# Scaling the attention weights by 1/sum on ScalarE, two units at a time, in place of a product on TensorE behind the values

## The chip, the cores and the metric

The kernel runs on one core of a Trainium2 chip. The core has five engines with queues of their own: TensorE (PE in the profile; PEld is its weight load), VectorE (DVE), ScalarE (ACT), GpSimd (POOL) and SyncE (SP, which issues the DMAs). The metric is the device time of one execution in microseconds (us). The kernel before took 731.99 us, the median of three runs from 730.23 to 732.29. One profiled execution of it took 733.05 us, and its profiled span is 731.3 us.

## The reference

Attention with four sink tokens and a window of 128, followed by a feed forward with a squared ReLU. The attention's output, its 8 heads side by side, is the feed forward's input.

```python
scores = scale * np.matmul(q, k.transpose(0, 1, 3, 2))   # q, k, v: (4, 8, 768, 64)
keep = is_sink | in_window          # pos < 4, or 0 <= row - pos < 128
scores = np.where(keep, scores, -1000000000.0)
scores = scores - np.max(scores, axis=-1, keepdims=True)
a = np.exp(scores)
a = a / (np.sum(a, axis=-1, keepdims=True) + 1e-09)
attn = np.matmul(a, v)              # then heads side by side: x is (3072, 512)
h = x @ w_in                        # w_in: (512, 2048), w_out: (2048, 512)
r = np.maximum(h, 0.0)
g = s * (r * r) + b
return g @ w_out
```

## The kernel before

**Chunks.** The 3072 tokens are worked in 8 chunks of 384 tokens, half a sequence each, in the order `ORDER`. For each chunk the attention is computed and then the feed forward. While the feed forward of chunk c runs, the attention of chunk c+1 is issued between its steps. Chunks 0 and 1 take their attention from a class of its own (`Plain`), which has its own normalisation; chunks 2 to 7 are built by `attn_slots`, and it is those that are meant by "from the third chunk on".

**Exactness by splits.** Products that must be exact to more bits than one pass of TensorE keeps are made of several: a value is cast to a rounded part and a rest (`kh` and `kl`, the two parts of `hl`, `x[0]` and `x[1]`, the two parts of `g`), and the products of the parts are added up in PSUM. So one feed-forward step is either 12 products `h<-x,w` of 128x384 (l1, line 608) or 9 products `po<-w,g` of 128x512 (l2, line 628), 16 steps of each kind per chunk, in turn.

**Units.** `attn_slots` cuts a chunk's attention into 24 units, one per head and block of 128 queries. A slot t issues the pieces of several units at different stages: the scores of unit t (`unit_a`: two products at lines 309 and 310, the mask, scale and negative maximum on DVE at 314, the exponential with its sum on ACT at 320, on POOL the addition at 323 of two 128x128 squares of the tile `sm` into one, and at 324 a copy of the sinks' exponentials into the tile `psk`); the transpose of unit t+1-LB into the spare columns of a PSUM bank (`turn`, line 330); the split of unit t-LB (`unit_b`: 343 on DVE, 345 on ACT, 346 on POOL); and the values' products of unit t-LC (`unit_c`: lines 375 and 383, and per head 390 and 391). LB is 4 and LC is 7, so a unit's transpose comes three slots behind its scores.

**Where 1/sum comes in.** The transposes and values' products work on exponentials that are not yet divided. Per pair of heads, behind the pair's last `unit_b`, 1/sum is computed on DVE for six columns (355 to 359) and written into spare columns of `psk`. `psk` of four heads is transposed (`ts`, 398) and copied to `xsk` (400, 401). From it `sinks` computes the sinks' part of the output (product `os`, 407; addition 408), and `scaled` spreads 1/sum over the rows with a constant selector (product `zb` with `sel`, 414) and multiplies the output with it on DVE (415), after which 416 and 417 split it for the feed forward.

**The order.** The slots of a chunk are spread over the feed forward's 32 steps: a step is issued, then slots as long as `i * (len(steps) - 2) < (j + 1) * len(slots)`. There are 33 slots for 30 places, so three steps take two slots each. The tile framework then sets each engine's queue from this text and its own estimates; an instruction that is wrapped in `tc.keep_in_program_order` keeps its place relative to the others so wrapped. Each engine works its queue in order. PSUM has five banks in the pool `psA` (scores with transposes, `h`, `o`, `ts`, `os`, `zb`) and three for `po`.

Of the kernel before, what the change touches and what calls it, by code (L numbers as in the profile page):

```python
# [15 lines left out]
P = 128  # L16
B, H, S, D = 4, 8, 768, 64
ORDER = ((0, 0), (1, 0), (0, 1), (1, 1), (2, 0), (2, 1), (3, 0), (3, 1))
NS = 8
# [18 lines left out]
LB, LC, LD, LDL, L2 = 4, 7, ((3, 4), (6, 7)), ((2, 2), (3, 3)), 2  # L38
# [3 lines left out]
def tile_kernel(ctx, tc, qT, kT, k0, v, vsk, n_sink, window, w, s, b, out):  # L42
# [46 lines left out]
    sel = const.tile([P, 2, P], F32R, tag="sel", name="sel")  # L89

# [43 lines left out]
    def constants2():  # L134

        spread = wk.tile([P, 2, P], F32, tag="y", name="spread", bufs=3)
        nc.gpsimd.memset(spread, 0.0)
        for j in range(4):
            row = spread[96:P, j // 2].rearrange("p (a d) -> p a d", a=2)
            nc.gpsimd.affine_select(out=row, in_=row, pattern=[[1, 2], [0, D]], compare_op=ALU.not_equal, fill=1.0,  # L140
                                    base=2 * j, channel_multiplier=-1)
        nc.scalar.copy(sel, spread)
# [102 lines left out]
    def load_pair(k, pr):  # L245
# [15 lines left out]
        pp.zz = wk.tile([P, BLK, 2], F32, tag="zz", name="zz", bufs=2)  # L261
# [36 lines left out]
    def unit_a(k, h, i, sc):  # L298
# [10 lines left out]
        nc.tensor.matmul(sc[:, :n], hd.qs[:, qs], hd.kh[:, c0:c0 + n], start=True, stop=False)  # L309
        nc.tensor.matmul(sc[:, :n], hd.qs[:, qs], hd.kl[:, c0:c0 + n], start=False, stop=True)  # L310
# [7 lines left out]
        s0 = k.cc[(h, i)][3]  # L318
        hh = h % 2
        nc.scalar.activation(sm[:, :n], sm[:, :n], AF.Exp, bias=negm[:, uu], scale=-1.0, accum_out=pp.zz[:, i, hh:hh + 1])  # L320
        if g > 0:
            c1, p1 = k.cc[(h, i)][1:3]
            nc.gpsimd.tensor_tensor(out=sm[:, c1:c1 + P], in0=sm[:, p1:p1 + P], in1=sm[:, c1:c1 + P], op=ALU.add)  # L323
        nc.gpsimd.tensor_copy(out=pp.psk[:, i, :12 * NS].rearrange("p (t x) -> p t x", t=3)[:, :, h % 4 * NS:(h % 4 + 1) * NS],  # L324
                              in_=sm[:, s0:s0 + NS].unsqueeze(1).to_broadcast([P, 3, NS]))

    def turn(k, h, i, tp):

        sm, c0 = k.cc[(h, i)][:2]
        nc.tensor.transpose(tp, sm[:, c0:c0 + P], ident)  # L330

    def unit_b(k, h, i, tp):
# [17 lines left out]
        pp = k.pairs[h // 2]  # L350
        if h % 2 == 1 and i == BLK - 1:
            z0 = 12 * NS + h // 2 % 2 * 4
            zr = wk.tile([P, 2, BLK, 2], F32, tag="zr", name="zr")
            zh = wk.tile([P, BLK, 2], F32R, tag="zh", name="zh")
            nc.vector.tensor_scalar(out=zr[:, 0], in0=pp.zz, scalar1=1e-9, scalar2=None, op0=ALU.add)
# [63 lines left out]
    def attn_slots(c):  # L419
# [16 lines left out]
        def slot(t):  # L436
            def f():
# [9 lines left out]
                if 0 <= t - LB < n:  # L447
                    unit_b(k, *units[t - LB], k.bank[:, 3 * P:])
# [399 lines left out]
```

## Time and profile before

| | |
|---|---|
| three runs, us | 732.29, 730.23, 731.99 |
| profiled execution, us | 733.05 |
| its span, us | 731.3 |
| matmuls on PE | 3812, 96% busy |
| DVE, ACT, POOL busy | 69%, 65%, 56% |
| products of the feed forward (608 and 628) | 297.7 and 299.1 us busy |
| DMA | 52.62 MB, mean 72 GB/s |

A row of instructions names the line, the engine, the operation and out<-in by the program's names. Matmuls are pipelined: one that is listed with 343 ns starts well before the one ahead of it has its end listed, so what a product costs PE is read from the distance between starts, and not from its duration. The feed forward of chunk 0 starts at about 44.5 us; the weights are still being prepared until about 123 us, and from 150.8 us on the stages repeat: one feed forward of some 82 to 86 us each (starts at 150.8, 237.0, 322.3, 404.7, 490.0, 572.3 and 657.0), the last of them without attention beside it.

### The profile page before, as it was taken

The numbers are of one execution on the slowest core, as the hardware profiler recorded it, in microseconds if no ns is written. First come the engines' busy times: TensorE is split into PE (matmuls) and PEld (weight loads), VectorE is DVE, ScalarE is ACT, GpSimd is POOL, SyncE is SP. The second block draws the span as 40 slices with busy tenths as digits, with TensorE's granted clock in tenths as the row PEclk, the third lists the DMA queues.
The fourth block names the chain that finished last, engine by engine and source line by source line (L and its number), as shares of the span: only waits on it lengthen the run. The fifth ranks groups of instructions, "written<-read, shape, count | busy, mean of one in ns | idle before, by whom it ended". The sixth has DMA issues, their size and how long they took to land.

```text
span 731.3 us, 11917 instructions
## 1 busy us (share of the span) xinstructions
PE 700.8 (96%) x3812; PEld 617.5 (84%) x3812; DVE 508.2 (69%) x1202; ACT 473.5 (65%) x1157; POOL 410.8 (56%) x703
## 2 busy tenths in 40 slices
PE   7599898999999999999999999999999999999996
PEld 4267666889988999899998999899999999989895
DVE  6969988548985788657786588847787589743331
ACT  6978877467774687656784677747775577633222
POOL 2556886348892588716674488915765389810000
PEclk8889988999999999999999999999999999999999
DMA  7845031131210212111111222111111212000001
GB/s 289 333 173 216 12 137 37 52 103 48 89 56 24 90 56 63 34 62 54 45 58 49 75 70 63 45 51 51 57 52 56 72 42 69 3 19 26 0 1 48
DMA packets 27381, 52.62 MB, mean 72 GB/s; under 512 B 3504, under 2 KB 15536, under 8 KB 25392
## 3 DMA queue, kind: packets, MB, share of 16 engines
q1 hardware_dynamic: 27312, 51.79, 21.3%
q8 instruction: 32, 0.52, 0.3%
q14 instruction: 37, 0.30, 0.1%
HBM read 45.49 MB, written 6.29 MB: 71 GB/s over the span
## 4 chain that ended last, share of the span: by engine, by line
PE 78%; DVE 9%; POOL 7%; ACT 3%; issue 2%; DMA 0%; SPq 0%; POOLq 0%; ACTq 0%; DVEq 0%
PE h L608 32%; PE po L628 32%; POOL w L206 4%; PE o L383 3%; PE sc L309 2%; PE sc L310 2%; PE sc L330 2%; DVE w L220 1%; PE tp L550 1%; PE o L561 1%; DVE smf L538 1%; DVE wt L219 1%; PE o L375 1%; POOL hl L346 1%; POOL kl L290 1%
## 5 line engine op out<-in xcount | busy, mean ns | idle before, releaser
L608 PE MATMUL h<-x,w 128*128 128x384 f32 x1536 | 297.7, 343 | 6.7 <-ACT tf L552 3.4
L628 PE MATMUL po<-w,g 128*128 128x512 f32 x1152 | 299.1, 405 | 0.0
L608 PEld LDWEIGHTS h<-x,w 128*128 128x128 f32 x1536 | 266.4, 189 | 13.1 <-ACT tf L552 3.8
L628 PEld LDWEIGHTS po<-w,g 128*128 128x128 f32 x1152 | 211.9, 191 | 45.6 <-issue 2.1
L614 DVE SCALAR_TENSOR_TENSOR r<-h,sb,r 128x384 f32<-128x384 f32 x112 | 68.9, 615 | 78.8 <-ACT r L611 77.7
L611 ACT ACTIVATE r<-h 128x384 f32<-128x384 f32 x128 | 62.6, 489 | 91.8 <-PE h L608 82.6
L617 DVE SCALAR_TENSOR_TENSOR g<-r,sb,g 128x384 fp32r<-128x384 f32 x112 | 91.1, 814 | 31.1 <-ACT g L616 29.6
L346 POOL TENSOR_TENSOR hl<-two,hl 128x256 fp32r<-128x256 f32 x128 | 102.3, 800 | 15.5 <-ACT hl L345 12.9
L323 POOL TENSOR_TENSOR sm<-sm 128x128 f32<-128x128 f32 x128 | 67.3, 526 | 60.9 <-ACT sm L320 59.1
L320 ACT ACTIVATE sm<-sm,negm 128x264 f32<-128x264 f32 (+1 forms) x144 | 72.1, 501 | 28.6 <-DVE negm L314 27.3
L616 ACT ACTIVATE g<-r,sb 128x384 fp32r<-128x384 f32 x112 | 69.1, 617 | 22.7 <-DVE r L614 22.0
L290 POOL TENSOR_TENSOR kl<-kraw,kh 128x528 fp32r<-128x528 f32 (+1 forms) x48 | 60.3, 1257 | 19.1 <-ACT kh L288 18.8
L206 POOL TENSOR_TENSOR w<-w 128x256 int32<-128x256 int32 x60 | 45.0, 780 | 40.3 <-DVE w L220 32.0
L345 ACT CAST hl<-two 128x256 fp32r<-128x256 f32 x128 | 50.5, 395 | 25.8 <-DVE two L343 25.5
L343 DVE TENSOR_TENSOR two<-sc,split 128x256 f32<-128x256 f32 x128 | 53.1, 417 | 5.8 <-POOL hl L346 5.5
L324 POOL COPY psk<-sm 128x24 f32<-128x24 f32 x144 | 35.5, 246 | 17.1 <-ACT sm L320 17.0
L383 PE MATMUL o<-hl,vv 128*128 128x256 f32 (+1 forms) x256 | 44.3, 275 | 0.0
L383 PEld LDWEIGHTS o<-hl,vv 128*128 128x128 f32 x256 | 39.6, 188 | 3.2
L289 DVE TENSOR_TENSOR qs<-qraw,qs 64x384 fp32r<-64x384 f32 x48 | 39.6, 825 | 3.7 <-ACT qs L285 1.9
L314 DVE CUSTOM_DVE_ANT_0 sm<-sc,m_all 128x264 f32<-128x264 f32 x64 | 27.3, 426 | 21.2 <-PE sc L310 19.2
L314 DVE CUSTOM_DVE_ANT_0 sm<-sc,msk 128x264 f32<-128x264 f32 (+1 forms) x80 | 32.0, 400 | 14.1 <-PE sc L310 13.4
L309 PE MATMUL sc<-kh,qs 128*128 128x264 f32 (+1 forms) x144 | 41.6, 291 | 0.0
(138 smaller groups left out, 960.4 us busy)
## 6 DMA issues: line engine op xcount, KB each, us to landing
w<-in_w SPq DMA_DIRECT2D x15, 1024.0 KB, 8.8
kraw<-in_kT SPq DMA_DIRECT2D x32, 264.0 KB, 2.6
out<-ot SPq DMA_DIRECT2D x24, 256.0 KB, 2.0
qraw<-in_qT SPq DMA_DIRECT2D x24, 192.0 KB, 2.4
vraw<-in_v SPq DMA_DIRECT2D x16, 256.0 KB, 2.8
kraw<-in_kT SPq DMA_DIRECT2D x16, 200.0 KB, 2.5
vsraw<-in_vsk SPq DMA_DIRECT2D x24, 64.0 KB, 2.1
vraw<-in_v SPq DMA_DIRECT2D x8, 192.0 KB, 2.4
```

What stands on the lines that cost most here:

```text
L206: nc.gpsimd.tensor_tensor(out=out[q], in0=in0[q], in1=in1[q], op=op)
L290: nc.gpsimd.tensor_tensor(out=hd.kl[:, :kw], in0=hd.k[:, :kw], in1=hd.kh[:, :kw].bitcast(F32), op=ALU.subtract)
L320: nc.scalar.activation(sm[:, :n], sm[:, :n], AF.Exp, bias=negm[:, uu], scale=-1.0, accum_out=pp.zz[:, i, hh:hh + 1])
L323: nc.gpsimd.tensor_tensor(out=sm[:, c1:c1 + P], in0=sm[:, p1:p1 + P], in1=sm[:, c1:c1 + P], op=ALU.add)
L346: nc.gpsimd.tensor_tensor(out=lo, in0=both, in1=hi.bitcast(F32), op=ALU.subtract)
L383: nc.tensor.matmul(hd.o[:, q0:q0 + n * P], hd.vv[:, kb, :], hd.hl[:, t, c0 * P:(c0 + n) * P], start=(hd.n == 0), stop=(i == BLK - 1 and kb ...
L608: nc.tensor.matmul(h[:, :CH], weight[f][:, 0, wi, cc * P:(cc + 1) * P], x[xi][:, cc, :], start=(i == 0), stop=(i == 11))
L611: nc.scalar.activation(r, h[:, :CH], AF.Relu, scale=1.0 / WUP)
L614: nc.vector.scalar_tensor_tensor(out=hr, in0=h[:, :CH], scalar=sw_ap, in1=r, op0=ALU.mult, op1=ALU.mult)
L616: nc.scalar.activation(gg[:, 0, :], hr, AF.Identity, bias=b_ap, scale=1.0)
L617: nc.vector.scalar_tensor_tensor(out=gg[:, 1, :], in0=hr, scalar=b_ap, in1=gg[:, 0, :].bitcast(F32), op0=ALU.add, op1=ALU.subtract)
L628: nc.tensor.matmul(po[tb], gg[:, gi, tsl], weight[f][:, 1, wi, :], start=(f == 0 and i == 0), stop=(f == NF - 1 and i == 2))
```

## The change

1/sum no longer goes through TensorE. A new function `norm` is called in every even slot for the two units whose scores were issued in the two slots before. It computes 1/sum of those two units on DVE (an addition and a reciprocal over two columns), multiplies each unit's added 128x128 square by it in place on ScalarE, and on POOL the former copy of the sinks' exponentials into `psk` becomes a multiplication by the same factor. The transposes, the values' products and the sinks' product then work on divided weights. `scaled`, its 24 products and multiplications, the constant `sel`, and the six-column computation per pair are gone; the two lines that split the output move to the end of `sinks`. One slot per chunk is gone, so there are 32 slots for 30 places and two steps take two slots. All products of `attn_slots` and of the feed forward are wrapped in `tc.keep_in_program_order`: besides those shown, the values' products, the transposes of `psk` and the product `os`.

```diff
-LB, LC, LD, LDL, L2 = 4, 7, ((3, 4), (6, 7)), ((2, 2), (3, 3)), 2
+LB, LC, LD, LDL, L2 = 4, 7, (3, 5), (2, 2), 2
...
-    sel = const.tile([P, 2, P], F32R, tag="sel", name="sel")
...
-        spread = wk.tile([P, 2, P], F32, tag="y", name="spread", bufs=3)
-        nc.gpsimd.memset(spread, 0.0)
-        for j in range(4):
-            row = spread[96:P, j // 2].rearrange("p (a d) -> p a d", a=2)
-            nc.gpsimd.affine_select(out=row, in_=row, pattern=[[1, 2], [0, D]], compare_op=ALU.not_equal, fill=1.0,
-                                    base=2 * j, channel_multiplier=-1)
-        nc.scalar.copy(sel, spread)
...
-        pp.zz = wk.tile([P, BLK, 2], F32, tag="zz", name="zz", bufs=2)
+        pp.z = wk.tile([P, 3, 2 * BLK], F32, tag="zz", name="zz", bufs=2)
...
-        nc.tensor.matmul(sc[:, :n], hd.qs[:, qs], hd.kh[:, c0:c0 + n], start=True, stop=False)
-        nc.tensor.matmul(sc[:, :n], hd.qs[:, qs], hd.kl[:, c0:c0 + n], start=False, stop=True)
+        tc.keep_in_program_order(nc.tensor.matmul(sc[:, :n], hd.qs[:, qs], hd.kh[:, c0:c0 + n], start=True, stop=False))
+        tc.keep_in_program_order(nc.tensor.matmul(sc[:, :n], hd.qs[:, qs], hd.kl[:, c0:c0 + n], start=False, stop=True))
...
-        s0 = k.cc[(h, i)][3]
-        hh = h % 2
-        nc.scalar.activation(sm[:, :n], sm[:, :n], AF.Exp, bias=negm[:, uu], scale=-1.0, accum_out=pp.zz[:, i, hh:hh + 1])
+        nc.scalar.activation(sm[:, :n], sm[:, :n], AF.Exp, bias=negm[:, uu], scale=-1.0,
+                             accum_out=pp.z[:, 0, h % 2 * BLK + i:h % 2 * BLK + i + 1])
         if g > 0:
             c1, p1 = k.cc[(h, i)][1:3]
             nc.gpsimd.tensor_tensor(out=sm[:, c1:c1 + P], in0=sm[:, p1:p1 + P], in1=sm[:, c1:c1 + P], op=ALU.add)
-        nc.gpsimd.tensor_copy(out=pp.psk[:, i, :12 * NS].rearrange("p (t x) -> p t x", t=3)[:, :, h % 4 * NS:(h % 4 + 1) * NS],
-                              in_=sm[:, s0:s0 + NS].unsqueeze(1).to_broadcast([P, 3, NS]))
+
+    def norm(k, *two):
+
+        z = k.pairs[two[0][0] // 2].z
+        j0 = two[0][0] % 2 * BLK + two[0][1]
+        jj = slice(j0, j0 + 2)
+        nc.vector.tensor_scalar(out=z[:, 1, jj], in0=z[:, 0, jj], scalar1=1e-9, scalar2=None, op0=ALU.add)
+        nc.vector.reciprocal(out=z[:, 2, jj], in_=z[:, 1, jj])
+        for j, (h, i) in enumerate(two):
+            pp = k.pairs[h // 2]
+            sm, c0, _, s0 = k.cc[(h, i)]
+            rz = z[:, 2, j0 + j:j0 + j + 1]
+            nc.scalar.mul(sm[:, c0:c0 + P], sm[:, c0:c0 + P], rz)
+            nc.gpsimd.tensor_scalar(out=pp.psk[:, i, :12 * NS].rearrange("p (t x) -> p t x", t=3)[:, :, h % 4 * NS:(h % 4 + 1) * NS],
+                                    in0=sm[:, s0:s0 + NS].unsqueeze(1).to_broadcast([P, 3, NS]), scalar1=rz, scalar2=None, op0=ALU.mult)
 
     def turn(k, h, i, tp):
 
         sm, c0 = k.cc[(h, i)][:2]
-        nc.tensor.transpose(tp, sm[:, c0:c0 + P], ident)
+        tc.keep_in_program_order(nc.tensor.transpose(tp, sm[:, c0:c0 + P], ident))
...
-        pp = k.pairs[h // 2]
-        if h % 2 == 1 and i == BLK - 1:
-            z0 = 12 * NS + h // 2 % 2 * 4
-            zr = wk.tile([P, 2, BLK, 2], F32, tag="zr", name="zr")
-            zh = wk.tile([P, BLK, 2], F32R, tag="zh", name="zh")
-            nc.vector.tensor_scalar(out=zr[:, 0], in0=pp.zz, scalar1=1e-9, scalar2=None, op0=ALU.add)
-            nc.vector.reciprocal(out=zr[:, 1], in_=zr[:, 0])
-            nc.vector.tensor_copy(zh, zr[:, 1])
-            nc.gpsimd.tensor_copy(out=pp.psk[:, :, z0:z0 + 2], in_=zh.bitcast(F32))
-            nc.vector.tensor_tensor(out=pp.psk[:, :, z0 + 2:z0 + 4], in0=zr[:, 1], in1=zh.bitcast(F32), op=ALU.subtract)
...
         os_ = ps("os")
-        nc.tensor.matmul(os_[:, :CH], pp.vs, pp.xs, start=True, stop=True)
+        tc.keep_in_program_order(nc.tensor.matmul(os_[:, :CH], pp.vs, pp.xs, start=True, stop=True))
         nc.vector.tensor_tensor(out=pp.x, in0=os_[:, :CH], in1=pp.x, op=ALU.add)
-
-    def scaled(k, pr):
-
-        pp = k.pairs[pr]
-        zb = ps("zb")
-        nc.tensor.matmul(zb[:, :CH], sel[:, pr % 2], pp.xs, start=True, stop=True)
-        nc.vector.tensor_tensor(out=pp.x, in0=zb[:, :CH], in1=pp.x, op=ALU.mult)
         nc.scalar.copy(k.x[0][:, pr, :], pp.x)
         (nc.vector if pr == H // 2 - 1 else nc.gpsimd).tensor_tensor(out=k.x[1][:, pr, :], in0=pp.x, in1=k.x[0][:, pr, :].bitcast(F32), op=ALU.subtract)
...
-            for d, fn in zip((LD if pr < H // 2 - 2 else LDL)[pr % 2], (sinks, scaled)):
-                ends.setdefault(t + d, []).append((fn, pr))
+            ends.setdefault(t + (LD if pr < H // 2 - 2 else LDL)[pr % 2], []).append((sinks, pr))
...
                     unit_b(k, *units[t - LB], k.bank[:, 3 * P:])
+                if t % 2 == 0 and 0 < t <= n:
+                    norm(k, *units[t - 2:t])
                 for fn, pr in ends.get(t, ()):
                     fn(k, pr)
...
-        parts = [slot(t) for t in range(n + LC + LDL[1][1])]
+        parts = [slot(t) for t in range(n + LC + LDL[1])]
         parts.pop(n + LB)
...
-                    nc.tensor.matmul(h[:, :CH], weight[f][:, 0, wi, cc * P:(cc + 1) * P], x[xi][:, cc, :], start=(i == 0), stop=(i == 11))
+                    tc.keep_in_program_order(nc.tensor.matmul(h[:, :CH], weight[f][:, 0, wi, cc * P:(cc + 1) * P], x[xi][:, cc, :], start=(i == 0), stop=(i == 11)))
...
-                    nc.tensor.matmul(po[tb], gg[:, gi, tsl], weight[f][:, 1, wi, :],
-                                     start=(f == 0 and i == 0), stop=(f == NF - 1 and i == 2))
+                    tc.keep_in_program_order(nc.tensor.matmul(po[tb], gg[:, gi, tsl], weight[f][:, 1, wi, :],
+                                     start=(f == 0 and i == 0), stop=(f == NF - 1 and i == 2)))
```

TensorE in the feed forward of chunk 2, where the attention of chunk 3 runs beside it and a step takes two slots. Before, the scores (309, 310) of units 11, 12 and 13 with the transposes (330) of units 8, 9 and 10:

```order
L309 MATMUL sc<-kh,qs 128x264
L310 MATMUL sc<-kl,qs 128x264
L330 MATMUL sc<-identr,sm 128x128
L375 MATMUL o<-hl,vv 128x256
L383 MATMUL o<-hl,vv 128x256 x2
L309 MATMUL sc<-kh,qs 128x264
L310 MATMUL sc<-kl,qs 128x264
L330 MATMUL sc<-identr,sm 128x128
L628 MATMUL po<-w_627,g 128x512 x9
L309 MATMUL sc<-kh,qs 128x264
L310 MATMUL sc<-kl,qs 128x264
L330 MATMUL sc<-identr,sm 128x128
```

After, the scores (300, 301) of units 15, 16 and 17 with the transposes (333) of units 12, 13 and 14:

```order
L300 MATMUL sc<-kh,qs 128x264
L301 MATMUL sc<-kl,qs 128x264
L333 MATMUL sc<-identr,sm 128x128
L615 MATMUL po<-w_721,g 128x512 x9
L300 MATMUL sc<-kh,qs 128x264
L301 MATMUL sc<-kl,qs 128x264
L333 MATMUL sc<-identr,sm 128x128
L376 MATMUL o<-hl,vv 128x256 x2
L376 MATMUL o<-hl,vv 128x128 x2
L300 MATMUL sc<-kh,qs 128x264
L301 MATMUL sc<-kl,qs 128x264
L333 MATMUL sc<-identr,sm 128x128
```

The two slots that share a step were those of units 11 and 12, ahead of the second-layer products; they are now those of units 16 and 17, behind them. The last row of the lower list is the transpose of unit 14, whose square is now multiplied by 1/sum before it; between it and the scores of unit 15 stand one step's nine products, two slots' scores and a head's values.

VectorE at the same place. Before, from the square of the feed forward (614) ahead of the mask of unit 11 on (314; 343 is the split of a transposed unit, 355 to 357 the 1/sum of a pair of heads):

```order
L614 SCALAR_TENSOR_TENSOR r<-h,sb,r 128x384
L314 ISA sm,negm<-sc,m_all 128x264
L314 ISA negm 128x1
L343 TENSOR_TENSOR two<-sc,split 128x256
L314 ISA sm,negm<-sc,m_all 128x264
L314 ISA negm 128x1
L617 SCALAR_TENSOR_TENSOR g<-r,sb,g 128x384
L343 TENSOR_TENSOR two<-sc,split 128x256
L355 TENSOR_SCALAR zr<-zz 128x6
L356 RECIPROCAL zr<-zr 128x6
L357 CAST zh<-zr 128x6
L391 TENSOR_TENSOR y<-o,y 64x512
```

After, from the square of the feed forward (601) ahead of the mask of unit 15 on (305 the mask, 384 the values' addition, 604 the second part of `g`, 346 the split, 320 and 321 the new addition and reciprocal):

```order
L601 SCALAR_TENSOR_TENSOR r<-h,sb,r 128x384
L305 ISA sm,negm<-sc,m_all 128x264
L305 ISA negm 128x1
L384 TENSOR_TENSOR y<-o,y 64x512
L604 SCALAR_TENSOR_TENSOR g<-r,sb,g 128x384
L346 TENSOR_TENSOR two<-sc,split 128x256
L305 ISA sm,negm<-sc,msk 128x264
L305 ISA negm 128x1
L346 TENSOR_TENSOR two<-sc,split 128x256
L320 TENSOR_SCALAR zz<-zz 128x2
L321 RECIPROCAL zz<-zz 128x2
```

The 1/sum of units 14 and 15 stands behind the mask of unit 16 and the splits of units 11 and 12.

ScalarE at the same place. Before, from the relu of the feed forward (611) on to the exponential (320) of unit 12 (288 and 294 prepare a head, 616 is the first part of `g`):

```order
L611 ACTIVATE r<-h 128x384
L288 CAST kh<-kraw 128x528
L616 ACTIVATE g<-r,sb 128x384
L294 CAST vv<-vraw 128x4x64
L320 ACTIVATE sm,zz<-sm,negm 128x264
L345 CAST hl<-two 128x256
L390 COPY y<-o 64x512
L320 ACTIVATE sm,zz<-sm,negm 128x264
L345 CAST hl<-two 128x256
```

After, from the relu (598) on to the multiplications (326) of units 14 and 15 (309 the exponential, 348 the split, 285 and 383 a head's preparation and values, 603 the first part of `g`):

```order
L598 ACTIVATE r<-h 128x384
L285 CAST vv<-vraw 128x4x64
L383 COPY y<-o 64x512
L603 ACTIVATE g<-r,sb 128x384
L309 ACTIVATE sm,zz<-sm,negm 128x264
L348 CAST hl<-two 128x256
L309 ACTIVATE sm,zz<-sm,negm 128x264
L348 CAST hl<-two 128x256
L326 ACTIVATE sm<-sm,zz 128x128 x2
```

The two multiplications stand behind the exponential of unit 16 and the split of unit 12. In the chunks of a sequence's first half (chunks 4 and 6) they stand ahead of that exponential.

## Rows read from the trace of the kernel before

**Rows 1.** The page, whole span: busy us (share), instructions.

```profile
PE 700.8 (96%) x3812; PEld 617.5 (84%) x3812; DVE 508.2 (69%) x1202; ACT 473.5 (65%) x1157; POOL 410.8 (56%) x703
```

**Rows 2.** Windows: stretch, its us, each engine's busy us (instructions), clock, DMA.

```profile
237.00:322.30 85.30, 84.81 (x479) 77.76 (x478) 62.69 (x147) 57.88 (x150) 58.25 (x103) 1.00 0.19 56
322.30:404.70 82.40, 82.40 (x464) 75.55 (x463) 59.60 (x147) 55.09 (x150) 47.22 (x87) 1.00 0.19 57
...
265.00:275.00 10.00, 10.00 (x62) 9.18 (x61) 9.37 (x23) 9.19 (x24) 9.00 (x16) 1.00 0.27 75
255.00:295.00 40.00, 39.93 (x238) 36.90 (x237) 33.42 (x84) 31.85 (x86) 34.85 (x63) 1.00 0.20 59
```

**Rows 3.** Waits of PE from 150 us: us, times, longest.

```profile
PE h L608 <- DVE y L415: 2.0, 3, 1.1
```

**Rows 4.** Timeline, PE, end of a chunk's attention: start, us, instruction.

```profile
315.34 0.34 PE L407 MATMUL os<-xsk,vs 128*128 128x384 f32 x1
315.51 0.34 PE L414 MATMUL zb<-xsk,sel 128*128 128x384 f32 x1
315.69 2.26 PE L628 MATMUL po<-w,g 128*128 128x512 f32 x9
```

**Rows 5.** Groups of PE from 150 us on: busy, mean ns | idle before.

```profile
L414 PE MATMUL zb<-xsk,sel 128*128 128x384 f32 x24 | 8.1, 337 | 0.0
```

**Rows 6.** Groups of DVE, 237 to 322.3: busy, mean ns | idle before.

```profile
L391 DVE TENSOR_TENSOR y<-o,y 64x512 f32<-64x512 f32 x8 | 5.5, 686 | 0.1
...
L415 DVE TENSOR_TENSOR y<-zb,y 128x384 f32<-128x384 f32 x4 | 2.2, 553 | 0.1
```

**Rows 7.** Groups of ACT, the same stretch.

```profile
L345 ACT CAST hl<-two 128x256 fp32r<-128x256 f32 x24 | 9.5, 394 | 4.7 <-DVE two L343 4.7
...
L276 ACT CAST vs<-vsraw 128x128 fp32r<-128x128 f32 x4 | 1.1, 293 | 0.0
```

**Rows 8.** Groups of POOL, the same stretch.

```profile
L324 POOL COPY psk<-sm 128x24 f32<-128x24 f32 x24 | 5.6, 231 | 0.0
...
L393 POOL TENSOR_TENSOR y<-y 128x128 f32<-128x128 f32 x4 | 1.9, 464 | 5.5 <-DVE y L391 5.5
```

**Rows 9.** Timeline, PE, where a step takes two slots.

```profile
264.62 0.57 PE L383 MATMUL o<-hl,vv 128*128 128x256 f32 x4
265.03 0.34 PE L309 MATMUL sc<-kh,qs 128*128 128x264 f32 x1
...
266.06 2.35 PE L628 MATMUL po<-w,g 128*128 128x512 f32 x9
268.25 0.28 PE L309 MATMUL sc<-kh,qs 128*128 128x264 f32 x1
268.37 0.29 PE L310 MATMUL sc<-kl,qs 128*128 128x264 f32 x1
```

**Rows 10.** Timeline, DVE, the same place.

```profile
265.41 0.62 DVE L614 SCALAR_TENSOR_TENSOR r<-h,sb,r 128x384 f32<-128x384 f32 x1 [2.04 <-ACT r L611]
265.94 0.42 DVE L314 CUSTOM_DVE_ANT_0 sm<-sc,m_all 128x264 f32<-128x264 f32 x1
...
266.97 0.88 DVE L617 SCALAR_TENSOR_TENSOR g<-r,sb,g 128x384 fp32r<-128x384 f32 x1
267.78 0.41 DVE L343 TENSOR_TENSOR two<-sc,split 128x256 f32<-128x256 f32 x1
268.11 0.36 DVE L355 TENSOR_SCALAR zr<-zz 128x6 f32<-128x6 f32 x1
```

**Rows 11.** Timeline, PE, scores that a free DVE waits for.

```profile
279.48 0.28 PE L310 MATMUL sc<-kl,qs 128*128 128x264 f32 x1
```

**Rows 12.** Timeline, DVE, a mask behind them, later a 1/sum.

```profile
279.80 0.43 DVE L314 CUSTOM_DVE_ANT_0 sm<-sc,m_all 128x264 f32<-128x264 f32 x1 [0.29 <-PE sc L310]
...
282.17 0.32 DVE L355 TENSOR_SCALAR zr<-zz 128x6 f32<-128x6 f32 x1
282.52 0.19 DVE L356 RECIPROCAL zr<-zr 128x6 f32<-128x6 f32 x1
```

More of the change, by code (lines that the diff above doesn't have):

```diff
@@ L374, in unit_c @@
             c0 = (2 * i + 1) * P
-            nc.tensor.matmul(hd.o[:, i * P:], hd.vv[:, cur, :], hd.hl[:, :, c0:c0 + P], start=False, stop=False)
+            tc.keep_in_program_order(nc.tensor.matmul(hd.o[:, i * P:], hd.vv[:, cur, :], hd.hl[:, :, c0:c0 + P], start=False, stop=False))
         if i > 0:
@@ L382, in unit_c @@
                 q0 = c0 // 2 * P
-                nc.tensor.matmul(hd.o[:, q0:q0 + n * P], hd.vv[:, kb, :], hd.hl[:, t, c0 * P:(c0 + n) * P],
-                                 start=(hd.n == 0), stop=(i == BLK - 1 and kb == cur - 1 and t == 1))
+                tc.keep_in_program_order(nc.tensor.matmul(hd.o[:, q0:q0 + n * P], hd.vv[:, kb, :], hd.hl[:, t, c0 * P:(c0 + n) * P],
+                                 start=(hd.n == 0), stop=(i == BLK - 1 and kb == cur - 1 and t == 1)))
                 hd.n += 1
@@ L397, in unit_c @@
                 for j in range(BLK):
-                    nc.tensor.transpose(ts[:, j * P:(j + 1) * P], pp.psk[:, j, :], ident)
+                    tc.keep_in_program_order(nc.tensor.transpose(ts[:, j * P:(j + 1) * P], pp.psk[:, j, :], ident))
                 pp.xs = k.pairs[h // 2 - 1].xs = wk.tile([P, CH], F32R, tag="xsk", name="xsk", bufs=1)
```

## The prediction

> **What bounds the kernel now.** I read the page's busy times first, then the windows by stage, then the waits of TensorE, and last the timelines of single places. The page has PE 96% busy and no other engine above 69% [rows 1]. By stage it is plainer: of the 85.30 us of one feed forward with attention beside it, PE is busy 84.81, DVE 62.69, ACT 57.88, POOL 58.25; of the next, 82.40 of 82.40 [rows 2]. The clock is granted in full (1.00, the upper of the two levels). So from 150 us on what counts is how much work stands in PE's queue, and each us in which PE waits at a place where it did not wait before. The waits of PE name one thing there: three waits for DVE's line 415, 2.0 us together [rows 3]. Line 415 is the multiplication by 1/sum, which frees the bank of `zb`.
>
> The averages hide one stretch: between 265 and 275 us DVE is busy 9.37 of 10 us, ACT 9.19, POOL 9.00 [rows 2]. Around it, from 255 to 295, ACT has 31.85 of 40. The other engines keep up with PE there, with little to spare.
>
> **What goes from PE.** Chunks 2 to 7 have four pairs of heads each, so 24 products `zb` go [rows 5]. Their listed 337 ns is not their price, since products overlap: at the end of an attention `os` starts at 315.34, `zb` at 315.51, `po` at 315.69 [rows 4], so a 128x384 product costs PE 0.17 to 0.18 us. 24 x 0.175 = 4.2 us. The three waits go with line 415 [rows 3]: 2.0 us. What would be late next there is the bank of `os`, freed by an addition that DVE does in the same place as before; I add nothing for it. PE's gain is 6.2 us.
>
> **What goes and comes on the other engines.** On DVE, line 415 (553 ns, four per chunk, [rows 6]) and four six-column computations go, and twelve additions and reciprocals of two columns come, which I price as the ones at 282.17 and 282.52, 0.35 us from start to start and 0.19 us for the reciprocal [rows 12]. DVE has about as much work as before, 6 us per chunk either way. On POOL the copy into `psk` (231 ns) becomes a multiplication; nearest from both sides are that copy and a POOL addition of 128x128 at 464 ns [rows 8], so 0 to 5.6 us per chunk more; it has over 24 us idle per chunk [rows 2] and its result is wanted only by the transposes of `psk` at the end of two pairs. I take nothing for it. The building of `sel` lies in the first microseconds beside other work: nothing.
>
> On ACT 24 multiplications per chunk come. No row shows one with a factor per row; nearest are a 128x128 cast at 293 ns and a 128x256 cast at 394 ns [rows 7]. I take 0.29, being the same shape. A chunk's 24 add 7.0 us (9.5 at the upper end) to 57.88, which leaves ACT at three quarters.
>
> The Trainium skill's page "ScalarE: Activation LUTs", section "What ACT_TABLE_LOAD costs", says that an ACTIVATE takes 186 ns plus 0.833 ns per element of a row with immediates, and some 93 ns more for each operand that is a pointer per partition. By it a 128-column multiplication would take an estimated 386 ns, where the cast's row without a pointer has 293; each of the waits below would be 0.1 us longer and the time 0.6 us higher. I keep the row.
>
> **What comes onto PE's path.** Before, a unit's transpose needed the exponential and POOL's addition. Now the transpose of the even unit of two needs the odd unit's exponential, DVE's addition and reciprocal, and ACT's multiplication. Normally two steps lie between the odd unit's scores and that transpose: nine products cost 2.19 us [rows 9] (266.06 to 268.25), twelve of the other kind 12 x 0.175 = 2.1 us, with scores and values some 4.7 us or more. Once per chunk two slots share a step, and only one step lies between. By the order these are now units 16 and 17, so the pair that has little time is 14 and 15.
>
> Count from the start of the nine products behind unit 15's scores. PE: nine products 2.19; unit 16's scores start at 2.19 and 2.31 [rows 9] (268.25, 268.37) and end at 2.60; transpose 13 about 2.44; four values' products 0.41 [rows 9] (264.62 to 265.03); unit 17's scores another 0.25. Transpose 14 is due at about 3.1.
>
> DVE: in the kernel before unit 11's scores start at 265.03 [rows 9] and with their transpose take PE about 0.3 us, so 265.35 answers to the start of the count; 614 starts at 265.41 [rows 10], 0.06 behind it. An instruction begins 0.07 to 0.09 before the listed end of the one ahead [rows 10] (265.41 + 0.62 against 265.94, 266.97 + 0.88 against 267.78). So 614 at 0.06, mask 15 at 0.6, the values' addition (686 ns, [rows 6]) at 0.95, 617 at 1.55, split 11 at 2.35, mask 16 at 2.7. The mask could not have come before 2.64 either: in a place where DVE was free it starts at 279.80, 0.04 behind the end of the scores at 279.48 + 0.28 [rows 11, 12]. Then split 12 at 3.05, addition 3.4 [rows 10] (267.78 to 268.11), reciprocal 3.75, done 3.93. A hand-over is some 0.1: ACT multiplies from 4.0 to 4.3, PE transposes at 4.4. PE waits 1.3 us. With the multiplication at 0.39 it is 1.4; if the mask 16 finds DVE free and the addition slips ahead of nothing else, 1.1; if POOL's addition or ACT's queue comes last, 1.9. This holds in chunks 2, 3, 5 and 7: 4 x 1.3 = 5.2.
>
> In chunks 4 and 6 the order has addition and reciprocal straight behind split 11: addition 2.7, reciprocal done 3.2, multiplication until 3.6, transpose 3.7 against 3.1: 0.6, twice, 1.2 us.
>
> Behind a waiting multiplication stand on ACT the next exponential and the casts of `hl`; those have two steps until PE wants them. The last pair of a chunk (22 and 23) has a long DVE addition between its addition and reciprocal; I put 0.1 us on it in the same four chunks and a little on drift: 0.5 us together, between 0 and 3.
>
> **Order kept in the text.** The wrapped products stay where the slots put them; before, the framework could slip them past each other. PE's rows at the quoted place are the same kinds in the same pattern, moved by four units; PE had no idle time there to win or lose. In the first 150 us some of the weights' work on DVE and ACT moves past chunk 1's normalisation; the DVE queue there has the same instructions. I take nothing, and 1 us either way.
>
> **Sum.** 733.05 - 4.2 - 2.0 + 5.2 + 1.2 + 0.5 = 733.75 for an execution like the profiled one, whose time stands 1.06 us above the median of the three runs. Against that median: 732.7. What a measurement can tell from no change is about 0.3%, 2.2 us.
>
> **Rivals.** (A) The short place costs nothing: the addition of two columns finds its way earlier, since the DVE queue ahead of it empties while PE works on the nine products. Then only PE's gain is left: 733.05 - 6.2 = 726.9, 725.8 against the median. For it: PE is the full engine and everything else has a quarter or more idle [rows 2]. Against it: mask 16 can't start before its scores, and it stands ahead of the addition in the queue; two things in a row would have to be shorter than their rows.
>
> The Trainium skill's page "Perfetto Trace Analysis", section "Identifying the Most-Contended Engine", says to take the busiest engine first. By that rule, work that leaves PE for engines with room is won. This case's rows agree that PE is the busiest (84.81 of 85.30), and the rule stands behind rival A; it leaves out a chain that gets longer than the time between two steps.
>
> (B) ACT runs full in the dense stretch and holds PE back pair after pair. One slot takes 85.3/30 = 2.84 us, so 10 us hold 3.5 multiplications, 1.0 us at 0.29 and 1.4 at 0.39: 9.19 + 1.0 = 10.2, or 10.6 of 10. It decides as soon as the exponential of an odd unit slips so far that the usual 4.7 us are no longer enough. Taken over 40 us ACT has 31.85 + 14 x 0.29 = 35.9 of 40, which speaks against a lasting jam. If it comes, each chunk loses 0.5 to 1 us more in two or three pairs, with the short pair at 1.9: 733.05 - 6.2 + 4 x 1.9 + 2 x 1.2 + 6 x 0.7 = 741, 740 against the median.
>
> (C) Only PE's waits go elsewhere: 415's bank is not what was late, and the waits of rows 3 stay with another releaser. Then 2.0 us less is won: 734.7 against the median.
>
> **Chances.** The forecast with its stalls between 4.5 and 8 us: 0.42 (731 to 735, most of it within 2.2 us of the median). A, wholly or with stalls up to 4 us: 0.30. B: 0.22. C: 0.06. Faster by over 0.3% is A and a small part of the forecast: 0.33. Within 0.3% is most of the forecast and a little of C: 0.31. Slower is B, the upper part of the forecast and most of C: 0.36. The range reaches from A to B, 725.8 to 740; the forecast's own is 730.5 to 735.5.
>
> **What would show it.** PE without `zb` and about 4 us less busy. In the timeline of PE, once per chunk, a transpose that waits for ACT's multiplication by 1.3 us in chunks 2, 3, 5 and 7 and by half of it in 4 and 6, behind the scores of unit 17; no waits for DVE at the ends of chunks. The multiplication's duration, 0.29 or 0.39. For B: waits of transposes for ACT spread over several pairs per chunk, between 255 and 295 us and its like. For A: none. The forecast is wrong if those waits add up to less than 4 or more than 9 us, or if PE waits in the middle of a chunk for anything but a multiplication.

## The result, and the profile after

The changed kernel takes 740.69 us (median of five runs, 739.85 to 741.32) against 731.99 in the same session: 1.0117 times the time before, 95% interval 1.0104 to 1.0131. The forecast was 732.7 us, its range 725.8 to 740.0. The profiled execution took 739.85 us with a span of 738.0; the spans differ by 6.7 us, the medians by 8.7, so some 2 us of the medians' difference lie in the scatter between executions and can't be followed in the two traces.

Read by stages, from the start of the first product of one feed forward to that of the next, the two traces differ like this (us; the last feed forward is read to the start of its last product; e1_cast and e3_even are experiments below):

| stage | before | after | e1_cast | e3_even |
|---|---|---|---|---|
| to the feed forward of chunk 0 | 44.52 | 45.55 | 43.63 | 43.74 |
| feed forward of chunk 0 (weights still being prepared) | 106.24 | 110.08 | 105.97 | 106.06 |
| feed forwards of chunks 1 to 6 | 506.23 | 507.79 | 507.73 | 498.18 |
| feed forward of chunk 7 | 67.33 | 68.08 | 68.07 | 68.08 |
| from the start of the last product on | 6.98 | 6.50 | 6.60 | 6.64 |

4.9 us of the 6.7 come before chunk 1's feed forward, where the change was held to cost nothing; the stages that the prediction worked out (chunks 1 to 6) differ by 1.6 us, where it had 0.7, the last feed forward by 0.8, and what is behind it by -0.5.

The page's first part of the changed kernel, beside [rows 1]: PE has 24 products less, ACT and POOL more to do.

```profile
PE 694.6 (94%) x3788; PEld 611.7 (83%) x3788; DVE 494.9 (67%) x1226; ACT 515.1 (70%) x1300; POOL 430.6 (58%) x674
```

The changed kernel's windows for the feed forwards of chunks 0, 2 and 7 (columns as in [rows 2]). In the first PE is idle for 14.5 us of 110, in the second for 1.5; that second stage answers to the one in [rows 2] that is busy 84.81 of 85.30: there is less work and more idle time.

```profile
45.55:155.63 110.08, 95.57 (x482) 75.02 (x481) 83.94 (x162) 75.61 (x153) 68.36 (x84) 0.95 0.30 106
...
240.70:325.93 85.23, 83.73 (x476) 76.97 (x474) 62.21 (x151) 64.77 (x174) 62.22 (x99) 1.00 0.19 56
...
663.42:731.50 68.08, 67.31 (x338) 60.66 (x337) 19.95 (x33) 19.18 (x36) 0.00 (x0) 1.00 0.03 13
```

The waits of PE from 150 us on, after. The three waits of [rows 3] are gone; six transposes wait for the multiplication (line 326), two first-layer products for a split on DVE at the end of the attentions of chunks 4 and 6 (line 352), and one second-layer product in the last feed forward.

```profile
PE sc L333 <- ACT sm L326: 6.3, 6, 1.5
PE h L595 <- DVE hl L352: 2.4, 2, 1.2
PE po L615 <- ACT r L598: 0.8, 1, 0.8
```

**The short place.** The timeline of PE of the changed kernel where units 16 and 17 share a step, in chunk 3. The last transpose is unit 14's.

```profile
282.24 0.28 PE L300 MATMUL sc<-kh,qs 128*128 128x264 f32 x1
...
283.18 0.28 PE L301 MATMUL sc<-kl,qs 128*128 128x264 f32 x1
284.97 0.33 PE L333 MATMUL sc<-identr,sm 128*128 128x128 f32 x1 [1.50 <-ACT sm L326]
```

DVE at the same place: the mask of unit 16 (305), the split of unit 12 (346), the addition and the reciprocal (320, 321).

```profile
282.87 0.41 DVE L305 CUSTOM_DVE_ANT_0 sm<-sc,msk 128x264 f32<-128x264 f32 x1
...
283.22 0.41 DVE L346 TENSOR_TENSOR two<-sc,split 128x256 f32<-128x256 f32 x1
283.55 0.67 DVE L320 TENSOR_SCALAR zz<-zz 128x2 f32<-128x2 f32 x1
284.25 0.17 DVE L321 RECIPROCAL zz<-zz 128x2 f32<-128x2 f32 x1
```

ACT at the same place: the two multiplications.

```profile
284.51 0.69 ACT L326 ACTIVATE sm<-sm,zz 128x128 f32<-128x128 f32 x2 [0.22 <-DVE zz L321]
```

The chain runs as forecast: mask, split, addition, reciprocal, multiplication, transpose. From the mask to the transpose it takes 2.1 us, where 1.7 was forecast (mask 2.7, transpose 4.4): the addition stands 0.70 us ahead of the reciprocal instead of 0.35, and the rest is as priced.

The addition seems to be held by GpSimd; the traces show it, and no run tests it. POOL at the same place (349 is the rest of a unit's split):

```profile
283.46 0.73 POOL L349 TENSOR_TENSOR hl<-two,hl 128x256 fp32r<-128x256 f32 x1 [0.48 <-ACT hl L348]
```

It ends at 284.19, and the addition on VectorE, begun at 283.55, at 284.22. In the whole trace 41 of the 72 additions begin while such an instruction of POOL has over 0.1 us to go, and each of the 41 ends 0.02 to 0.03 us behind the end of that one, after 0.16 to 0.93 us. Of the other 31, 28 take 0.15 to 0.17 us; three take 0.77, and POOL begins one within 0.02 us of their start, as it does at six of the 28. In the kernel before all 24 additions of line 355 end in this way behind one of POOL's, so the 0.35 us of the forecast had such a wait in it already.

**What a wait costs.** A listed wait begins at the listed end of the product ahead; without the wait the next product would have started before that end. So the price of a wait is read here as the distance between the two starts, less the usual distance of two such products (the median in the same trace). The transpose at 284.97 starts 1.79 us behind the product at 283.18, where 0.13 is usual: it costs 1.66, and 1.50 is listed. The second of the three waits of [rows 3], in the kernel before, costs 0.72 - 0.03 = 0.69, and 0.42 is listed:

```profile
302.57 0.30 PE L330 MATMUL sc<-identr,sm 128*128 128x128 f32 x1
303.29 2.36 PE L608 MATMUL h<-x,w 128*128 128x384 f32 x12 [0.42 <-DVE y L415]
```

At these prices (of every delay above 0.11 us) the feed forwards of chunks 1 to 6 hold 3.7 us of waits before: 2.8 behind line 415 and 0.9 in four short ones of transposes. After, they hold 10.6: 7.3 for the multiplication, 3.0 for the split and 0.4 in two short ones. What is left of the 506.2 and 507.8 us without them is 502.6 and 497.2. Of the kernels below it is 502.0 to 502.7 in those with the product `zb` and 497.1 to 497.8 in those without it (499.5 in e4_imm, which has 16.5 us of waits), so the 24 products cost some 5 us.

**The first 150 us.** The waits of PE during the feed forward of chunk 0, before (8.2 us in all):

```profile
PE sc L510 <- DVE g L617: 3.4, 3, 2.2
PE h L608 <- ACT tf L552: 3.4, 2, 2.2
PE h L608 <- DVE g L617: 1.4, 1, 1.4
```

The longest ones after (13.2 of 14.4 us):

```profile
PE sc L497 <- DVE g L604: 6.7, 2, 6.2
PE tp L537 <- ACT tf L539: 3.5, 1, 3.5
PE po L615 <- ACT g L603: 1.6, 1, 1.6
PE h L595 <- ACT tf L539: 1.4, 1, 1.4
```

The longest one in the timeline of PE, after (the scores of chunk 1's own attention):

```profile
95.61 0.91 PE L497 MATMUL sc<-kf,qf 64*128 64x384 f32 x2
102.77 1.65 PE L497 MATMUL sc<-kf,qf 64*128 64x384 f32 x2 [6.25 <-DVE g L604]
```

Before, the same scores waited 2.16 us, and on DVE the second part of the feed forward's `g` (617) stood ahead of the second part of a weight (231):

```profile
93.15 1.64 PE L510 MATMUL sc<-kf,qf 64*128 64x384 f32 x2 [2.16 <-DVE g L617]
```

```profile
92.49 0.60 DVE L617 SCALAR_TENSOR_TENSOR g<-h,sb,g 128x384 fp32r<-128x384 f32 x1
...
96.47 1.62 DVE L231 TENSOR_TENSOR w<-w,w 128x1024 fp32r<-128x1024 f32 x1 [1.16 <-POOL w L206]
```

DVE there after: line 222, the second part of a weight, stands ahead of line 604 and waits for POOL.

```profile
96.90 0.61 DVE L601 SCALAR_TENSOR_TENSOR h<-h,sb,r 128x384 f32<-128x384 f32 x1
100.57 1.62 DVE L222 TENSOR_TENSOR w<-w,w 128x1024 fp32r<-128x1024 f32 x1 [3.06 <-POOL w L197]
102.11 0.60 DVE L604 SCALAR_TENSOR_TENSOR g<-h,sb,g 128x384 fp32r<-128x384 f32 x1
```

No instruction of the new 1/sum lies there. What has changed is the order: in the queues of DVE, ACT and POOL the pieces that prepare the weights stand in other places among the attention of chunk 1.

### The profile page after: what moved, and what is told of

Its sections match the earlier page's. It is cut to its first block, busy times and chain, and to the rows that moved or that the text cites. A ratio compares the mean times of both kernels' runs of the same rounds, so it can differ in the third digit from the quotient of the medians.

```text
span 738.0 us, 12010 instructions
## 1 busy us (share of the span) xinstructions
PE 694.6 (94%) x3788; PEld 611.7 (83%) x3788; DVE 494.9 (67%) x1226; ACT 515.1 (70%) x1300; POOL 430.6 (58%) x674
## 4 chain that ended last, share of the span: by engine, by line
PE 66%; DVE 13%; ACT 12%; POOL 4%; issue 3%; DMA 1%; SPq 0%; ACTq 0%; DVEq 0%; POOLq 0%
PE h L595 28%; PE po L615 27%; POOL w L197 4%; PE o L376 3%; PE sc L333 2%; PE sc L300 2%; PE sc L301 2%; DVE qs L280 2%; DVE g L604 1%; ACT r L598 1%; ACT w L217 1%; ACT sm L326 1%; ACT sm L309 1%; ACT g L603 1%; PE tp L537 1%
## 5 line engine op out<-in xcount | busy, mean ns | idle before, releaser
L615 PE MATMUL po<-w,g 128*128 128x512 f32 x1152 | 295.5, 402 | 2.4 <-ACT g L603 1.6
L349 POOL TENSOR_TENSOR hl<-two,hl 128x256 fp32r<-128x256 f32 x128 | 97.8, 766 | 10.8 <-ACT hl L348 10.6
L604 DVE SCALAR_TENSOR_TENSOR g<-r,sb,g 128x384 fp32r<-128x384 f32 x112 | 76.8, 686 | 37.1 <-ACT g L603 36.0
L327 POOL TENSOR_SCALAR psk<-sm,zz 128x24 f32<-128x24 f32 x144 | 59.5, 428 | 10.1 <-DVE zz L321 8.8
L326 ACT ACTIVATE sm<-sm,zz 128x128 f32<-128x128 f32 x144 | 51.3, 395 | 7.0 <-DVE zz L321 6.4
L280 DVE TENSOR_TENSOR qs<-qraw,qs 64x384 fp32r<-64x384 f32 x48 | 48.9, 1019 | 9.4 <-ACT qs L276 8.4
L286 POOL TENSOR_TENSOR vv<-vraw,vv 128x256 fp32r<-128x256 f32 (+1 forms) x48 | 33.3, 696 | 36.2 <-ACT vv L285 35.8
L333 PE MATMUL sc<-identr,sm 128*128 128x128 f32 x144 | 40.1, 278 | 6.4 <-ACT sm L326 6.3
```

Of the source, the lines that this page charges most:

```text
L280: nc.vector.tensor_tensor(out=hd.qs[other], in0=hd.q, in1=hd.qs[hd.half].bitcast(F32), op=ALU.subtract)
L349: nc.gpsimd.tensor_tensor(out=lo, in0=both, in1=hi.bitcast(F32), op=ALU.subtract)
L604: nc.vector.scalar_tensor_tensor(out=gg[:, 1, :], in0=hr, scalar=b_ap, in1=gg[:, 0, :].bitcast(F32), op0=ALU.add, op1=ALU.subtract)
L615: tc.keep_in_program_order(nc.tensor.matmul(po[tb], gg[:, gi, tsl], weight[f][:, 1, wi, :], start=(f == 0 and i == 0), stop=(f == NF - 1 a ...
```

## The experiments

Theory after the result: **S**, the order of the weights' work was changed by something in the change, and costs 4.9 us; **T**, in the repeating stages PE pays at the one place per chunk where two slots share a step, and not by a load on ScalarE. Rivals: **K**, the products kept in the text's order delay the start; **B**, ScalarE is full (the prediction's second rival).

**e1_cast.** What was the first operation of ScalarE before the change, the cast into `sel`, was put back into the changed kernel with a memset on GpSimd for its input; nothing uses it.

```diff
+    sel = const.tile([P, 2, P], F32R, tag="sel", name="sel")
...
     def constants2():
 
+        spread = wk.tile([P, 2, P], F32, tag="y", name="spread", bufs=3)
+        nc.gpsimd.memset(spread, 0.0)
+        nc.scalar.copy(sel, spread)
```

> The changed kernel, with the former first instruction of ScalarE (memset of a scratch tile and its cast into the unused constant sel) put back and nothing else. Theory S: this one cast sets the framework's order of the weights' work, and that order costs 4.9 us before the feed forward of chunk 1. Then that feed forward starts at 150.8 us as before the change (not 155.6), and the time is 740.7 - 4.9 = 735.8 us. Rival K: the products kept in the text's order delay the start; then nothing changes, 740.7 us and a start at 155.6.

Measured: 733.86 us, 1.0033 times before (1.0013 to 1.0054), 1.9 less than expected. Chunk 1's feed forward starts at 149.6 us; everything behind it takes as long as after the change (table). So S holds and K falls: one cast and its memset, of which nothing uses the result, are worth 6.0 us in the trace. The first 291 instructions on DVE and the first 241 on ACT, up to 154 us, stand in the order of the kernel before; in the changed kernel, without the cast, DVE leaves that order with its 7th instruction. A window of e1_cast, the feed forward of chunk 0:

```profile
43.63:149.60 105.97, 96.18 (x482) 75.92 (x481) 83.90 (x162) 78.16 (x155) 68.34 (x84) 0.95 0.31 110
```

**e2_sellate.** The reverse in the kernel before: the same constant is built where chunk 1 begins.

```diff
     def constants2():
 
-        spread = wk.tile([P, 2, P], F32, tag="y", name="spread", bufs=3)
-        nc.gpsimd.memset(spread, 0.0)
...
-        nc.scalar.copy(sel, spread)
...
             for t in psks:
                 nc.gpsimd.memset(t, 0.0)
+            spread = wk.tile([P, 2, P], F32, tag="y", name="spread", bufs=3)
+            nc.gpsimd.memset(spread, 0.0)
...
+            nc.scalar.copy(sel, spread)
```

> The kernel before, with the building of the constant sel moved to where chunk 1 begins, so that its cast is no longer the first instruction of ScalarE; products unpinned, 1/sum as before. Theory S: the feed forward of chunk 1 starts near 155.6 instead of 150.8 us and the time is 732.0 + 4.9 = 736.9 us. Rival K: nothing changes, 732.0 us, a start at 150.8.

Measured: 738.45 us, 1.0096 (1.0074 to 1.0118). Chunk 1's feed forward starts at 156.35, and from there to the last product it is 573.41 us against 573.56 before. The window of chunk 0's feed forward in e2_sellate is as long as that of the changed kernel to 0.1 us, its engines are busy as long to 0.3, and PE has the long wait of the changed kernel, without anything of the change in it:

```profile
46.21:156.35 110.14, 95.77 (x482) 75.20 (x481) 83.98 (x162) 75.90 (x154) 68.28 (x84) 0.95 0.30 106
```

```profile
PE sc L503 <- DVE g L610: 6.4, 2, 6.2
```

DVE's first 291 instructions stand in the order of the changed kernel. Over all twelve kernels of this document, chunk 1's feed forward starts at 149.6 to 151.3 us in the nine with the early cast and at 155.6 to 156.4 in the three without it. The cast and its memset were always moved together, so which of the two sets the order is open.

**e3_even.** e1_cast, with the steps of two slots at other places.

```diff
-            while i < len(slots) and i * (len(steps) - 2 * (c > 0)) < (j + 1) * len(slots):
+            while i < len(slots) and (i * len(steps) < (j + 1) * len(slots) if c == 0 else i < j + 2 + (j >= 25)):
```

> e1_cast with another spread of the 32 slots over 30 places in chunks 2 to 7: the steps that take two slots are the first one (units 0 and 1) and the 26th (slots 26 and 27, which have no scores). Theory T: PE waits for the multiplication only where two slots share a step in the middle; the six waits of 6.3 us go, and the time is 735.8 - 6.3 = 729.5 us. Rival B: ScalarE is full in the dense stretch; the waits for it move to other units, stay above 4 us in sum, and the time stays above 733.

Measured: 725.11 us, 0.9917 (0.9896 to 0.9938): faster than both kernels. It gained more than the 6.3 us expected, 9.6 us in chunks 1 to 6 against e1_cast, since the two waits behind the split on DVE went as well and each wait costs more than is listed (at the prices above 10.6 us in e1_cast, 0.6 in e3_even). The waits of PE from 150 us on in e3_even:

```profile
PE po L620 <- ACT r L603: 0.8, 1, 0.8
PE sc L338 <- ACT sm L331: 0.6, 1, 0.6
```

ScalarE has the same 144 multiplications as in e1_cast, in less time. Rival B falls.

**e5_mid.** e1_cast with both steps of two slots in the middle of a chunk.

```diff
-            while i < len(slots) and i * (len(steps) - 2 * (c > 0)) < (j + 1) * len(slots):
+            while i < len(slots) and (i * len(steps) < (j + 1) * len(slots) if c == 0 else i < j + 1 + (j >= 8) + (j >= 15)):
```

> e1_cast with the two steps of a chunk that take two slots put at slots 8 and 9 and at slots 16 and 17 (e1_cast has them at 0 and 1 and at 16 and 17). Theory T: each such step in the middle leaves only one step between an odd unit's scores and the transpose of its partner, so each costs a wait for the multiplication; twelve waits in place of six, 10 to 13 us in place of 6.2, and 738 to 740 us. Rival B (a full ScalarE or any other steady load): the waits don't follow the place of those steps, 734 us as e1_cast.

Measured: 743.43 us, 1.0161 (1.0144 to 1.0178), a few us beyond what was expected. The waits for the multiplication double:

```profile
PE sc L338 <- ACT sm L331: 13.3, 13, 1.7
```

That they follow the steps is shown. The place at slots 8 and 9 costs about as much as the one at 16 and 17: 1.68 us listed against 1.53 in chunk 2, 1.30 against some 1.53 in chunks 3, 5 and 7, 0.41 against 0.23 in 4 and 6. Most of what went beyond the expectation is that a wait costs more than is listed: the 13 come to 15.4 us by the distances between starts, where e1_cast's six are 7.1.

**e4_imm.** The multiplication without its wait for the reciprocal.

```diff
-            nc.scalar.mul(sm[:, c0:c0 + P], sm[:, c0:c0 + P], rz)
+            nc.scalar.mul(sm[:, c0:c0 + P], sm[:, c0:c0 + P], 0.5)
```

> e1_cast with the multiplication on ScalarE by the constant 0.5 in place of 1/sum (so 1/sum is left out of the weights); it waits for POOL's addition and no longer for the reciprocal. Theory T: the chain over DVE's reciprocal is what PE waits for, the waits fall from 6.3 to under 1 us and the time is near 729.8 us. Rival B: ScalarE's work itself is late, waits stay above 4 us, 734 to 736 us. The multiplication lists 0.29 us in place of 0.395 if the factor per row is what made it longer than a cast of the same shape.

Measured: 742.86 us, 1.0147 (1.0113 to 1.018). This one missed: no transpose waits for the multiplication any more, but the framework set other queues for the new dependence. ACT now waits for POOL's addition in front of every other multiplication, and PE waits in other places, 4.1 us for the values' addition alone. As a test of the chain it says nothing. The wait of ACT in chunk 3's attention:

```profile
ACT sm L331 <- POOL sm L318: 9.5, 13, 1.7
```

It does settle the price of the factor. The multiplication by a constant in e4_imm:

```profile
L331 ACT ACTIVATE sm<-sm 128x128 f32<-128x128 f32 x24 | 7.4, 309 | 9.8 <-POOL sm L318 9.5
```

and by a factor per row in the changed kernel, with the cast of the same shape behind it:

```profile
L326 ACT ACTIVATE sm<-sm,zz 128x128 f32<-128x128 f32 x24 | 8.4, 394 | 1.2 <-DVE zz L321 1.1
...
L267 ACT CAST vs<-vsraw 128x128 fp32r<-128x128 f32 x4 | 1.1, 294 | 0.0
```

**e7_keep.** The kernel before with its products kept in the text's order; each is wrapped as in the change, `zb` too.

```diff
-        nc.tensor.matmul(zb[:, :CH], sel[:, pr % 2], pp.xs, start=True, stop=True)
+        tc.keep_in_program_order(nc.tensor.matmul(zb[:, :CH], sel[:, pr % 2], pp.xs, start=True, stop=True))
...
```

> The kernel before with all its products kept in the text's order and nothing else. Theory: nothing but the 0.75 us of the last feed forward, 732.7 us. Rival K: the keeping by itself costs several us, 735 us or more.

Measured: 734.13 us, 1.0024 (1.0014 to 1.0034), 1.4 more than expected. The last feed forward takes 68.14 us, as in the changed kernel, and chunks 1 to 6 take 507.23, 1.0 more, all of it in the feed forwards of chunks 3 and 5, where a transpose now waits 0.3 us for the square of the feed forward (line 614). Its start is that of the kernel before (150.81), the second sign against K.

**e6_unpin.** e3_even without keeping any product; the wraps of the change are taken off again.

```diff
-                    tc.keep_in_program_order(nc.tensor.matmul(h[:, :CH], weight[f][:, 0, wi, cc * P:(cc + 1) * P], x[xi][:, cc, :], start=(i == 0), stop=(i == 11)))
+                    nc.tensor.matmul(h[:, :CH], weight[f][:, 0, wi, cc * P:(cc + 1) * P], x[xi][:, cc, :], start=(i == 0), stop=(i == 11))
...
```

> e3_even with none of the products kept in the text's order. If the keeping matters only by the 0.75 us that the last feed forward takes longer than before (68.08 against 67.33 us), 724.4 us; if it is what keeps the waits away in the middle, waits of PE come back and it takes 727 us or more; if it does nothing, 725.1.

Measured: 725.43 us, 0.9914 (0.9898 to 0.9931), as e3_even. The last feed forward is back at 67.55 us; the runs can't tell the half microsecond.

**e8_nozb.** The kernel before without the product `zb` and the multiplication behind it; the output is left undivided.

```diff
-        zb = ps("zb")
-        nc.tensor.matmul(zb[:, :CH], sel[:, pr % 2], pp.xs, start=True, stop=True)
-        nc.vector.tensor_tensor(out=pp.x, in0=zb[:, :CH], in1=pp.x, op=ALU.mult)
```

> The kernel before without the product zb and the multiplication behind it (so the output isn't divided by the sums), 1/sum still computed: the gain on PE alone. The prediction put it at 4.2 for the products and 2.0 for the waits, so 725.7 us; by the stages of e3_even, which gain 8.0 us in all (573.56 to 566.26, and 0.75 given back in the last one), it is 724.

Measured: 724.99 us, 0.9902 (0.9886 to 0.9919). In chunks 1 to 6 it gains 506.23 - 498.86 = 7.4 us, and from 150 us on PE has no wait listed (by the distances between starts, 1.1 us of short ones). This is about what the change could gain on PE; e3_even gains 8.0 there.

**e9_pacebefore.** The spread of e3_even in the kernel before.

```diff
-            while i < len(slots) and i * (len(steps) - 2 * (c > 0)) < (j + 1) * len(slots):
+            while i < len(slots) and (i * len(steps) < (j + 1) * len(slots) if c == 0 else i < j + 2 + (j >= 25) + (j >= 28)):
```

> The kernel before with the spread of e3_even (its 33 slots over 30 places: two slots in the first, the 26th and the 29th step), 1/sum still by the product zb. Theory T: before has no chain that the place of those steps could break, so only the 2 to 3 us of waits behind line 415 can change; 729 to 733 us. Rival: the spread by itself is what made e3_even faster, 725 us or less.

Measured: 733.68 us, 1.0018 (1.0008 to 1.0028): the spread gains nothing by itself. The waits behind line 415 go, and four transposes wait 3.0 us for the values' addition (line 391) instead.

**e10_evennocast.** e3_even without the cast at the start.

```diff
-    sel = const.tile([P, 2, P], F32R, tag="sel", name="sel")
...
-        spread = wk.tile([P, 2, P], F32, tag="y", name="spread", bufs=3)
-        nc.gpsimd.memset(spread, 0.0)
-        nc.scalar.copy(sel, spread)
```

> The changed kernel with the spread of e3_even and without the cast at the start. Theory S and T add up: 725.1 + 5 to 6 us = 730 to 731 us, a start of chunk 1's feed forward at 155 to 156 us. Rival: the order at the start costs less once the rest is not late, under 728 us.

Measured: 731.03 us, 0.9985 (0.9973 to 0.9997). The start is at 155.89, chunks 1 to 6 take 498.22. The two causes add up.

## Why the prediction was wrong, by its steps

**The step that failed** is "In the first 150 us some of the weights' work on DVE and ACT moves past chunk 1's normalisation; the DVE queue there has the same instructions. I take nothing, and 1 us either way." It costs 4.9 us in the trace (chunk 1's feed forward at 155.63 instead of 150.76), 6.0 by e1_cast and 5.6 by e2_sellate. The same instructions in another order are not the same time where each engine works in order and PE already waits for DVE: a weight's second part that waits 3.06 us for POOL holds the feed forward's line 604 behind it, and PE 6.25 us. The prediction also called the building of `sel` hidden, "nothing". Its duration is hidden (the next operation of ScalarE starts at 7.8 us in both traces), but its presence sets the order. Added to the forecast of 732.7, 4.9 gives 737.6, inside the range. The other 3.1 us to the measured 740.69 are 0.9 in chunks 1 to 6, 0.8 in the last feed forward, -0.5 behind it, and 1.9 of scatter between the executions.

**PE's gain** was mis-sized: 6.2 forecast, 7.4 by e8_nozb. The waits for line 415 cost 2.8 us by the distances between starts, where the listed 2.0 was taken, short waits of transposes for 0.9 us were left out, and the 24 products cost some 5 us instead of 4.2.

**The short place** was right in its mechanism, its chunks and its units: six waits, listed with 6.3 us. That this meets the 6.4 forecast (5.2 + 1.2) is luck. The prediction counted from the start that was due to the start that came; so counted the waits are 1.6 to 1.7 us in chunks 2, 3, 5 and 7 (1.3 forecast), 0.4 in 4 and 6 (0.6 forecast), and 7.3 in sum. The transpose was due at 3.1 us, as forecast; it was the addition that ended late, together with POOL's instruction. e5_mid and e3_even show that it is the place of the shared step that counts.

**The multiplication** takes 394 ns, the upper bound; the 293 ns chosen from the cast was too low by the factor per row (309 with a constant). Here the trace agrees with the Trainium skill, page "ScalarE: Activation LUTs", section "What ACT_TABLE_LOAD costs": the prediction's estimate from it, 386 ns, was set aside. POOL's copy with a factor takes 428 ns where the copy took 246 (means over all chunks); as forecast, PE does not wait for it.

**What would be late next** at the bank of line 415 was put at nothing; the two waits for a split on DVE at the ends of chunks 4 and 6 are listed with 2.4 us and cost 3.0, against the prediction's "no waits for DVE at the ends of chunks". e3_even, with the order kept, doesn't have them, so they too hang on the spread. Whether the kept order has a part in them is open: e7_keep loses 0.5 us in each of the same two stages, but in another wait some 4 us earlier, and the changed kernel with its own spread was not run unpinned.

**Order kept in the text** was put at nothing and costs 1.8 us in the kernel before (e7_keep: 1.0 in chunks 1 to 6, 0.8 in the last). In the changed kernel the 0.8 us of the last feed forward is there too, a second-layer product that waits for the relu; the rest is not shown.

Of the rivals, B named a time near the measured one (740) for a reason that isn't there: the waits for ScalarE are the six that were forecast, and not spread over the dense stretch. C isn't it either: PE waited for line 415 at the ends of the attentions of chunks 2, 3 and 5, and for the split at those of 4 and 6.

In sum, from the first product of chunk 1 to that of chunk 7 and by the distances between starts: -5.4 outside the waits (the products), -3.7 for the waits that went, +10.6 for those that came, measured +1.6. The forecast of +0.7 was near it by luck too: the gains were 2.9 us larger than worked out and the losses 3.7.

## What to carry to other kernels

Where a framework sets the queues, compare the queues of the whole program before and after an edit, not only around it: a constant that is no longer built, here with the first operation of an engine, can reorder a stage that has nothing to do with the edit. Price such a stage by who is bound there, and put back what held the order, here one cast with its memset, to see its worth. Where work is moved from a full engine into a chain of others, look for the place with the least time between the chain's ends, and move the schedule's irregular steps away from it; here this and the cast together turned 1.2% slower into 0.8% faster than before, and without the cast it made 0.15% faster (e10_evennocast). Price a wait by the distance between starts, not by its listed length.

## What the runs showed that was not expected

A cast whose result nobody uses is worth, with its memset, some 6 us (e1_cast, e2_sellate), through the order alone; why the framework orders the weights otherwise without it was not found. The addition on 128x2 lists 0.67 us at the short place, where one on 128x6 took 0.32 to 0.36 before [rows 10, 12] and one with POOL idle takes 0.15; in the rows it ends with POOL's instruction beside it. In the changed kernel the waits cost PE 0.16 to 0.30 us each beyond what is listed. The factor per row costs ScalarE 85 ns (394 against 309) at 128x128.
